# A fused attention, expert and SoLU kernel: w_gate split in six steps, weight conversion one chunk later, and other PSUM banks for the last block's first matmul

## The chip, the cores and the metric

The kernel runs on one core of a Trainium2 chip. The metric is the device time of one execution in microseconds, and runs are compared by their median. The engines are named as in the profile: PE (matmul) with PEld (its weight loads), DVE (VectorE), ACT (ScalarE), POOL (GpSimd) and SP, which here issues the DMAs. Each engine works through its own queue in order: an instruction that waits holds everything behind it on that engine.

## The reference, cut to what matters

Three layers follow each other. Attention with random features works on 4 batches, 8 heads, 576 positions and 128 features. Its output x (2304 tokens by 512) goes through a gate that picks one of 8 experts for each token. The result goes through a SoLU layer.

```python
def _attn_ref(q, k, v, omega):
    q_p, k_p = phi(q_s), phi(k_s)              # exp of a projection less its maximum
    kv = np.einsum('bhsm,bhsd->bhmd', k_p, v)
    num = np.einsum('bhsm,bhmd->bhsd', q_p, kv)
    return num / den

def _moe_ref(x, w_gate, w1, w2):
    logits = x @ w_gate
    expert_idx = np.argmax(logits, axis=1)
    for e in range(E):
        h = np.maximum(xe @ w1[e], 0.0)
        out[mask] = gate_w[mask, None] * (h @ w2[e])

def _moe2_ref(x, w_in, w_out, g_ln):
    h = x @ w_in                               # then softmax * h, layer norm
    return (ln @ w_out).astype(np.float32)
```

## The kernel before, in words

Every fp32 operand of a large matmul is split into two fp16 parts, high and low, and a product is three matmuls: high by high, high by low, low by high. ACT makes the high part, DVE or POOL the low part by a subtraction.

The work has three strands, each a Python generator whose pieces are placed by hand in the order of the program. Strand A (`stream_a`) is the attention: units of 128 positions and half of the heads, pipelined over a few units. A unit's projection `pj` goes to PSUM, DVE takes its negative maximum `nm` (L213), ACT takes the exponential `feat` (L219), and DVE and ACT split it into `fh` and `fl`. Strand B (`phase_b(b)`, b from 0 to 3) computes one batch's expert layer, under the assumption that all its tokens take the expert of its first token (a fallback repairs the tokens that do not). Its first matmul, here called g1, has 16 passes of 12 matmuls; each pass fills one PSUM bank with 128 by 288 results, which ACT writes as `hh` (L646) and DVE as the remainder `hl` (L647). Its second matmul, g2, has 8 passes of 24 matmuls, whose results ACT writes to `yT` (L652). Strand C is the SoLU layer at the end, whose first two tiles (`c_start`) start inside block 3.

Before strand B begins, strand A runs alone for some slots (a slot is one unit of strand A). A table `pre` hangs other work on single slots, among it `wg_split` on slot 9: it scales w_gate by its largest absolute value (over partitions by a matmul with a tile of ones, `wgs`) and splits it into `wg`, which the routing matmul `rt` (L337) reads in later slots.

The weights of strand C come as 64-bit words. Sixteen chunks of 128 by 512 are loaded (`craw`), repacked to 32 bits by three DVE instructions (L606, L607, L609, into `ctmp`), scaled by ACT (L625), rounded by ACT (L626, `wih` or `woh`), and the remainder is made by POOL (L62, `wil` or `wol`). `craw` and `ctmp` have two buffers each. `cw_split(k)` does this in three steps, and one step is taken after each step of strand B from the middle of block 2 on. The order within one step of strand B is: the PE pass, the evacuation of the pass before it (`flush`), the splitting of expert weights (`wh` L557, `wl` L558), then the step of `cw_split`, and in block 3 what `first_c` holds (`y_early` makes `yc` on ACT and POOL).

Banks for g1 and g2 come from `b_bank`. Once strand A has ended it alternates two pools of two banks, so a pass waits for the evacuation of the pass four before it:

```python
        if cps and count[0] % 2:
            return cps["t"].tile([128, cs.stop - cs.start], F32, name=name, tag="lt")
        return bpsum.tile([128, cs.stop - cs.start], F32, name=name, tag="b")
```

Passes of block 3's g1 are numbered 0 to 15 below, and hh(n) and hl(n) are the evacuation of pass n. They are issued after the matmuls of pass n+1.

Of the kernel before, what the change touches and what calls it, by code (L numbers as in the profile page):

```python
# [8 lines left out]
F32 = mybir.dt.float32  # L9
# [4 lines left out]
AF = mybir.ActivationFunctionType  # L14
# [6 lines left out]
B, H, S, D, M = 4, 8, 576, 64, 128  # L21
# [35 lines left out]
def f32(ap):  # L57
    return ap.bitcast(F32)


def sub(eng, out, a, b):
    eng.tensor_tensor(out=out, in0=a, in1=b, op=ALU.subtract)  # L62
# [3 lines left out]
def attn_moe_solu(ctx: ExitStack, tc, qk0, qT, kT, v, omT, w_gate, w1, w2, w_in, w_out, g_ln, out):  # L66
    nc = tc.nc
    pe, act, dve, pool, sp = nc.tensor, nc.scalar, nc.vector, nc.gpsimd, nc.sync
# [98 lines left out]
    def split_v(b, t):  # L167

        r = vparts[b, t] = vraws.pop((b, t))
        if t < 4:  # L170
            act.activation(v_h[:, t, :, 0:64], r, AF.Copy, scale=VS)
        else:
            for o in range(2):
                p, hs = slice(64 * o, 64 * o + 64), slice(4 * o, 4 * o + 4)
                act.activation(v_h[p, t, hs, 0:64], r[p, hs], AF.Copy, scale=VS)

    def split_v_lo(b, t):
        r = vparts.pop((b, t))
        if t < 4:
            dve.scalar_tensor_tensor(v_l[:, t], r, VS, v_h[:, t, :, 0:64], op0=ALU.mult, op1=ALU.subtract)  # L180
        else:
            for o in range(2):
                p, hs = slice(64 * o, 64 * o + 64), slice(4 * o, 4 * o + 4)
                dve.scalar_tensor_tensor(v_l[p, t, hs], r[p, hs], VS, v_h[p, t, hs, 0:64],
                                          op0=ALU.mult, op1=ALU.subtract)
# [374 lines left out]
    def pump(limit, due=0):  # L560

        state["calls"] += 1
        while state["split"] < min(limit, state["dma"]):
            i = state["split"]
            if i >= due and state["calls"] - sent[i] < 2:
                break
            chunk_split(i)
            state["split"] += 1
        while state["dma"] < min(max(state["split"] + NRAW, 8), len(chunks)) and chunks[state["dma"]][0] in ereg:
            chunk_dma(state["dma"])  # L570
            sent[state["dma"]] = state["calls"]
            state["dma"] += 1
# [3 lines left out]
    cs_ = {}  # L576
    rooms = {}
# [15 lines left out]
    def cw_dma(k):  # L593
        if k >= 16:
            return
        if k < 8:
            c, hf = divmod(k, 2)
            src = w_in[c * 128:c * 128 + 128, hf * 512:hf * 512 + 512]
        else:
            src = w_out[(k - 8) * 128:(k - 8) * 128 + 128, :]  # L600
        sp.dma_start(cs_["raw"][:, k % 2], src.bitcast(I32).rearrange("p (f t) -> p f t", t=2))

    def words32(w, raw):

        lo, hi = raw[:, :, 0], raw[:, :, 1]
        dve.tensor_scalar(w, hi, 3, 0x3FFFFFF8, op0=ALU.logical_shift_left, op1=ALU.bitwise_and)  # L606
        dve.scalar_tensor_tensor(w, hi, -0x40000000, w, op0=ALU.bitwise_and, op1=ALU.bitwise_or)  # L607
        yield
        dve.scalar_tensor_tensor(w, lo, 29, w, op0=ALU.logical_shift_right, op1=ALU.bitwise_or)  # L609

    def cw_split(k):

        if k < 8:
            c, hf = divmod(k, 2)
            h, l = [cw[n][:, c, hf * 512:hf * 512 + 512] for n in ("wih", "wil")]
            g = WS
        else:
            h, l = [cw[n][:, k - 8, :] for n in ("woh", "wol")]
            g = g_ws[:, k - 8:k - 7]
        w = cs_["w"][:, k % 2]  # L620
        yield from words32(w, cs_["raw"][:, k % 2])
        cw_dma(k + 2)
        yield
        w = f32(w)
        act.activation(w, w, AF.Copy, scale=g)  # L625
        act.copy(h, w)  # L626
        sub(pool, l, w, h)
        yield

    cps = {}  # L630
    count = [0]

    def b_bank(b, name, cs):
        count[0] += 1
        if cps and count[0] % 2:
            return cps["t"].tile([128, cs.stop - cs.start], F32, name=name, tag="lt")
        return bpsum.tile([128, cs.stop - cs.start], F32, name=name, tag="b")

    def phase_b(b):
        xh, xl = xTs[b]  # L640
        hh = bp.tile([128, 8, S], F16, name="hh", tag="hh")
        hl = bp.tile([128, 8, S], F16, name="hl", tag="hl")
        todo = []

        def evac_h(ps, ft, cs):
            act.activation(hh[:, ft, cs], ps, AF.Relu)  # L646
            dve.scalar_tensor_tensor(hl[:, ft, cs], ps, 0.0, hh[:, ft, cs], op0=ALU.max, op1=ALU.subtract)  # L647

        def evac_y(ps, dt, cs):
            if dt == 0 and cs.start == 0:  # L650
                yTs[b] = ypool.tile([128, 4, S], F32, name="yT", tag=f"y{b}")
            act.activation(yTs[b][:, dt, cs], ps, AF.Copy, scale=YS / (XS * BS * BS))  # L652

        def flush():
            while todo:
                todo.pop(0)()

        c0 = 16 * b
        halves = (slice(0, 256), slice(256, S)) if b == 0 else (slice(0, HS), slice(HS, S))
        if b == 0:  # L660
            passes = [(ft, cs) for cs in halves for ft in range(8)]
        else:
            passes = [(ft, cs) for ft in range(8) for cs in halves]
        for n, (ft, cs) in enumerate(passes):
            if (b, ft) not in wt:
                pump(c0 + ft + 1, c0 + ft + 1)
            wh, wl = wt[b, ft]
            ps = b_bank(b, "g1", cs)
            for c in range(4):
                pe.matmul(ps, wh[:, c, :], xh[:, c, cs], start=(c == 0), stop=False)  # L670
                pe.matmul(ps, wh[:, c, :], xl[:, c, cs], start=False, stop=False)  # L671
                pe.matmul(ps, wl[:, c, :], xh[:, c, cs], start=False, stop=(c == 3))  # L672
            flush()
            todo.append(lambda ps=ps, ft=ft, cs=cs: evac_h(ps, ft, cs))
            pump(c0 + ft + 5 if b else (n + 3 if n < 6 else 9 + max(0, n - 12)))
            yield
        for dt in range(4):
            if (b, 9 + 2 * dt) not in wt:
                pump(c0 + 10 + 2 * dt, c0 + 10 + 2 * dt)
            ww = [wt[b, 8 + 2 * dt], wt[b, 9 + 2 * dt]]  # L680
            for s, cs in enumerate(halves):
                ps = b_bank(b, "g2", cs)
                for k in range(8):
                    wh, wl = ww[k // 4]
                    if k == 7:
                        flush()
                    pe.matmul(ps, wh[:, k % 4, :], hh[:, k, cs], start=(k == 0), stop=False)  # L687
                    pe.matmul(ps, wh[:, k % 4, :], hl[:, k, cs], start=False, stop=False)  # L688
                    pe.matmul(ps, wl[:, k % 4, :], hh[:, k, cs], start=False, stop=(k == 7))  # L689
                    if k == 3:  # L690
                        flush()
                        pump(c0 + 8 + 2 * dt + 5)
                        yield
                todo.append(lambda ps=ps, dt=dt, cs=cs: evac_y(ps, dt, cs))
                pump(c0 + 8 + 2 * dt + 5 + s)
                yield
        flush()
# [342 lines left out]
    for o in range(2):  # L1040
        p, cs = slice(64 * o, 64 * o + 64), slice(128 * o, 128 * o + 128)
# [12 lines left out]
        if live[0] and next(a, a) is a:  # L1054
            live[0] = False

    def wg_split():

        dve.tensor_reduce(lgs[:, 0:1], wg_raw, axis=AX.XY, op=ALU.max, apply_absolute_value=True)
        ps = bpsum.tile([128, 512], F32, name="wgs", tag="b")  # L1060
        pe.matmul(ps[:, 0:1], ones, lgs[:, 0:1], start=True, stop=True)
        dve.tensor_scalar(lgs[:, 1:2], ps[:, 0:1], 2.0 ** -14, 1e-30, op0=ALU.mult, op1=ALU.max)
        dve.reciprocal(lgs[:, 0:1], lgs[:, 1:2])
        dve.tensor_scalar(wg_raw, wg_raw, lgs[:, 0:1], None, op0=ALU.mult)
        dve.tensor_scalar(lgs[:, 1:2], lgs[:, 1:2], 1.0 / XS, None, op0=ALU.mult)
        dve.tensor_copy(wg[:, 0], wg_raw)
        dve.tensor_tensor(wg[:, 1], wg_raw, wg[:, 0], op=ALU.subtract)

    split_v(0, 0)
    pre = {0: lambda: (split_pair(0, "k", 2), split_v_lo(0, 0), load_v(0, 3), split_v(0, 1)),  # L1070
           1: lambda: (split_pair(0, "k", 3), split_v_lo(0, 1), load_v(0, 4), split_v(0, 2)),
           2: lambda: (split_pair(0, "k", 4), split_v_lo(0, 2), split_v(0, 3)),
           3: lambda: (split_v_lo(0, 3), split_v(0, 4)),
           4: lambda: split_v_lo(0, 4),
           9: wg_split}
    slot = 0
    while x_done.get(0, -1) < 1:
        a_half()
# [15 lines left out]
    def c_start(k):  # L1094
# [4 lines left out]
    first_c = {3: lambda: y_early(0), 7: lambda: y_early(1), 11: lambda: y_early(2), 15: lambda: y_early(3),  # L1099
               23: lambda: c_start(0), 25: lambda: next(ms[0]), 26: lambda: next(ms[0]),  # L1100
               27: lambda: c_start(1), 29: lambda: next(ms[1]), 30: lambda: next(ms[1])}
    cwg = (_ for k in range(16) for _ in cw_split(k))
    for b in range(B):
        while b and x_done.get(b, -1) < 4:
            a_half()
# [88 lines left out]
```

## Time and profile before

| what | value |
|---|---|
| median of 3 runs | 562.1 us (561.03 to 564.17) |
| the profiled execution | 563.37 us, its span 561.5 us |
| busy share of the span | PE 90%, DVE 77%, ACT 60%, POOL 11% |
| chain that ended last | PE 50%, DVE 21%, ACT 11%, DMA 7% |

Sums about the change are made against the profiled execution: 561.5 us of span and 1.87 us outside it. That execution lies 1.3 us above the median. The 90% for PE is a mean over stages: in the first stage (strand A alone) PE is idle a good part of the time, in most of strand B and C it is busy throughout.

### The profile page before, as it was taken

How to read it: one execution, taken by the hardware profiler on the slowest of the kernel's cores; microseconds unless marked ns; L12 is line 12 of the kernel's file. 1: busy time of each engine (PE TensorE's matmuls, PEld its weight loads, DVE VectorE, ACT ScalarE, POOL GpSimd, SP SyncE). 2: the span in 40 equal slices, each digit the busy share in tenths (PEclk: the TensorE clock that was granted, in tenths of full speed). 3: DMA queues.
4: the chain of work that ended last, by engine and by line, in shares of the span. 5: the costliest groups of instructions: out<-in, count | busy, mean ns of one | idle time of the engine just before them, and what ended most of it. 6: DMA issues, size and time to landing. Idle time of an engine off the chain costs nothing.

```text
span 561.5 us, 11966 instructions
## 1 busy us (share of the span) xinstructions
PE 506.7 (90%) x4440; PEld 344.8 (61%) x4440; DVE 432.3 (77%) x926; ACT 339.3 (60%) x769; POOL 63.0 (11%) x86
## 2 busy tenths in 40 slices
PE   6878698797988999989989978999999999999995
PEld 2557576586867878868877756664444444444443
DVE  5978877588978988677886777767699988778670
ACT  6768468687777867666654564534474646655520
POOL 4210000000000000000012143221112121211200
PEclk8998989798999999999999999999999999999999
DMA  7405664626663455521556454505777776676741
GB/s 252 114 2 175 185 177 109 180 54 208 174 189 108 135 159 146 159 78 57 169 170 183 141 176 135 167 0 151 206 188 206 195 207 161 180 195 149 152 112 42
DMA packets 80143, 83.50 MB, mean 149 GB/s; under 512 B 43728, under 2 KB 50512, under 8 KB 80080
## 3 DMA queue, kind: packets, MB, share of 16 engines
q1 hardware_dynamic: 80080, 82.69, 51.9%
q8 instruction: 36, 0.59, 0.4%
q14 instruction: 27, 0.22, 0.1%
HBM read 56.71 MB, written 9.44 MB: 118 GB/s over the span
## 4 chain that ended last, share of the span: by engine, by line
PE 50%; DVE 21%; ACT 11%; DMA 7%; issue 6%; SPq 3%; POOL 1%; ACTq 0%; DVEq 0%; POOLq 0%
PE h L743 5%; PE o L810 5%; PE o L812 5%; PE o L811 5%; PE h L741 5%; PE h L742 5%; ACT feat L219 4%; DVE nm L213 4%; PE g L687 3%; PE g L688 3%; PE g L689 3%; PE g L670 2%; PE g L672 2%; PE g L671 2%; DMA vraw<-in_v_dram 2%
## 5 line engine op out<-in xcount | busy, mean ns | idle before, releaser
L219 ACT ACTIVATE feat<-pj,nm 128x128 f32<-128x128 f32 x288 | 82.7, 377 | 40.4 <-DVE nm L213 37.9
L670 PE MATMUL g<-xh,wh 128*128 128x288 f16 (+2 forms) x224 | 64.6, 288 | 12.3 <-DVE hl L647 11.7
L687 PE MATMUL g<-hh,wh 128*128 128x288 f16 (+2 forms) x256 | 74.3, 290 | 1.4 <-DVE hl L647 1.4
L688 PE MATMUL g<-hl,wh 128*128 128x288 f16 (+2 forms) x256 | 74.4, 290 | 0.4 <-DVE hl L647 0.4
L689 PE MATMUL g<-hh,wl 128*128 128x288 f16 (+2 forms) x256 | 74.4, 290 | 0.0
L672 PE MATMUL g<-xh,wl 128*128 128x288 f16 (+2 forms) x224 | 64.6, 288 | 0.0
L671 PE MATMUL g<-xl,wh 128*128 128x288 f16 (+2 forms) x224 | 64.6, 288 | 0.0
L810 PE MATMUL o<-woh,lh 128*128 128x512 f16 (+1 forms) x152 | 55.9, 368 | 0.3 <-ACT ob L813 0.3
L812 PE MATMUL o<-woh,ll 128*128 128x512 f16 (+1 forms) x152 | 55.9, 368 | 0.0
L811 PE MATMUL o<-wol,lh 128*128 128x512 f16 (+1 forms) x152 | 55.9, 368 | 0.0
L558 DVE SCALAR_TENSOR_TENSOR wl<-wraw,wh 128x512 f16<-128x512 f32 x56 | 42.3, 756 | 12.2 <-ACT wh L557 8.9
L213 DVE TENSOR_REDUCE nm<-pj 128x4 f32<-128x512 f32 x72 | 49.0, 681 | 1.9 <-PE pj L199 1.0
L743 PE MATMUL h<-wih,yl 128*128 128x512 f16 x112 | 42.5, 379 | 0.7 <-POOL yl L62 0.7
L647 DVE SCALAR_TENSOR_TENSOR hl<-g,hh 128x288 f16<-128x288 f32 (+2 forms) x64 | 28.8, 451 | 18.0 <-ACT hh L646 18.0
L741 PE MATMUL h<-wih,yh 128*128 128x512 f16 x112 | 42.5, 379 | 0.0
L742 PE MATMUL h<-wil,yh 128*128 128x512 f16 x112 | 42.4, 379 | 0.0
L237 DVE SCALAR_TENSOR_TENSOR fl<-feat,fh 128x512 f16<-128x512 f32 x36 | 27.3, 758 | 16.3 <-ACT fh L233 15.2
L62 POOL TENSOR_TENSOR wil<-ctmp,wih 128x512 f16<-128x512 f32 x8 | 9.3, 1158 | 272.2 <-ACT wih L626 272.2
L557 ACT ACTIVATE wh<-wraw 128x512 f16<-128x512 f32 x56 | 35.7, 638 | 3.6 <-PE g L688 3.6
L838 ACT ACTIVATE wck<-wck 128x2048 f32<-128x2048 f32 x16 | 30.5, 1904 | 12.2 <-DMA wck<-in_w_dram 12.2
L207 PE MATMUL pj<-ws,stk 128*128 128x128 f16 x216 | 31.3, 224 | 4.5 <-DMA stk<-hlp 3.4
L751 DVE TENSOR_REDUCE sc<-h 128x1 f32<-128x1024 f32 x18 | 21.9, 1218 | 16.8 <-PE h L743 16.8
(183 smaller groups left out, 1231.6 us busy)
## 6 DMA issues: line engine op xcount, KB each, us to landing
wck<-in_w_dram SPq DMA_DIRECT2D x16, 1024.0 KB, 6.0
wraw<-in_w_dram SPq DMA_DIRECT2D x56, 256.0 KB, 2.8
stk<-hlp SPq DMA_DIRECT2D x96, 72.0 KB, 2.3
out_dram<-ob SPq DMA_DIRECT2D x17, 256.0 KB, 2.2
vraw<-in_v_dram SPq DMA_DIRECT2D x16, 256.0 KB, 4.6
xd<-x SPq DMA_DIRECT2D x16, 256.0 KB, 3.5
craw<-in_w_in_dram SPq DMA_DIRECT2D x8, 512.0 KB, 4.1
craw<-in_w_out_dram SPq DMA_DIRECT2D x8, 512.0 KB, 3.3
```

The source lines that it names most:

```text
L213: dve.tensor_reduce(nm, ps, axis=AX.X, op=ALU.max, negate=True)
L219: act.activation(f[:, i, :], ps[:, i, :], AF.Exp, bias=nm[:, i:i + 1])
L670: pe.matmul(ps, wh[:, c, :], xh[:, c, cs], start=(c == 0), stop=False)
L671: pe.matmul(ps, wh[:, c, :], xl[:, c, cs], start=False, stop=False)
L672: pe.matmul(ps, wl[:, c, :], xh[:, c, cs], start=False, stop=(c == 3))
L687: pe.matmul(ps, wh[:, k % 4, :], hh[:, k, cs], start=(k == 0), stop=False)
L688: pe.matmul(ps, wh[:, k % 4, :], hl[:, k, cs], start=False, stop=False)
L689: pe.matmul(ps, wl[:, k % 4, :], hh[:, k, cs], start=False, stop=(k == 7))
L741: pe.matmul(ps[:, n, :], h[:, c, :], cw["wih"][:, c, cs], start=(c == 0), stop=False)
L810: pe.matmul(ps, h[:, k, :], cw["woh"][:, k, cs], start=(k == 0), stop=False)
L811: pe.matmul(ps, h[:, k, :], cw["wol"][:, k, cs], start=False, stop=False)
L812: pe.matmul(ps, l[:, k, :], cw["woh"][:, k, cs], start=False, stop=(k == 7))
```

## The change

The change has three parts. First, `wg_split` becomes a generator of six steps on slots 6 to 11. Second, `words32` gives up control after each of its DVE instructions, and the ACT and POOL part of a chunk's conversion is put on a list and issued in the second step of the next chunk; the load of the chunk after next moves to the third step. Third, in block 3 the passes 7, 9, 11, 13 and 15 of g1 take halves (one bank each) of two-bank tiles `h` of the pool that strand C uses for its own first matmul.

```diff
         dve.tensor_scalar(w, hi, 3, 0x3FFFFFF8, op0=ALU.logical_shift_left, op1=ALU.bitwise_and)
+        yield
         dve.scalar_tensor_tensor(w, hi, -0x40000000, w, op0=ALU.bitwise_and, op1=ALU.bitwise_or)
         yield
         dve.scalar_tensor_tensor(w, lo, 29, w, op0=ALU.logical_shift_right, op1=ALU.bitwise_or)
...
-        yield from words32(w, cs_["raw"][:, k % 2])
+        for _ in words32(w, cs_["raw"][:, k % 2]):
+            yield
+            for part in cw_parts:
+                cw_parts.pop()()
         cw_dma(k + 2)
-        yield
-        w = f32(w)
-        act.activation(w, w, AF.Copy, scale=g)
-        act.copy(h, w)
-        sub(pool, l, w, h)
-        yield
+
+        def parts():
+            wf = f32(w)
+            act.activation(wf, wf, AF.Copy, scale=g)
+            act.copy(h, wf)
+            sub(pool, l, wf, h)
+
+        cw_parts.append(parts)
+        yield
+
+    cw_parts = []
...
-    def b_bank(b, name, cs):
+    def b_bank(b, name, cs, spare=False):
         count[0] += 1
+        if cps and b == B - 1 and name == "g1" and spare:
+            if count[0] % 4 == 0:
+                rooms["g1"] = cps["h"].tile([128, 2, 512], F32, name="h")
+            if count[0] % 4 in (0, 2) and "g1" in rooms:
+                return rooms["g1"][:, count[0] % 4 // 2, 0:cs.stop - cs.start]
...
-            ps = b_bank(b, "g1", cs)
+            ps = b_bank(b, "g1", cs, n > 4)
...
-    def wg_split():
+    def wg_steps():
 
         dve.tensor_reduce(lgs[:, 0:1], wg_raw, axis=AX.XY, op=ALU.max, apply_absolute_value=True)
+        yield
         ps = bpsum.tile([128, 512], F32, name="wgs", tag="b")
         pe.matmul(ps[:, 0:1], ones, lgs[:, 0:1], start=True, stop=True)
+        yield
         dve.tensor_scalar(lgs[:, 1:2], ps[:, 0:1], 2.0 ** -14, 1e-30, op0=ALU.mult, op1=ALU.max)
         dve.reciprocal(lgs[:, 0:1], lgs[:, 1:2])
+        yield
         dve.tensor_scalar(wg_raw, wg_raw, lgs[:, 0:1], None, op0=ALU.mult)
+        yield
         dve.tensor_scalar(lgs[:, 1:2], lgs[:, 1:2], 1.0 / XS, None, op0=ALU.mult)
         dve.tensor_copy(wg[:, 0], wg_raw)
+        yield
         dve.tensor_tensor(wg[:, 1], wg_raw, wg[:, 0], op=ALU.subtract)
-
+        yield
+
+    wgs = wg_steps()
...
-           9: wg_split}
+           **{6 + k: lambda: next(wgs) for k in range(6)}}
...
-    cwg = (_ for k in range(16) for _ in cw_split(k))
+    def cw_all():
+        for k in range(16):
+            yield from cw_split(k)
+        yield
+        cw_parts.pop()()
+
+    cwg = cw_all()
```

On DVE, around slot 9 of the start, the order moves like this (`lgs` holds the maximum and its reciprocal, `wg_raw` is w_gate, `kvl` and `nm` belong to strand A):

```order
-L1059 TENSOR_REDUCE lgs<-wg_raw 128x1
-L1062 TENSOR_SCALAR lgs<-wgs 128x1
-L1063 RECIPROCAL lgs<-lgs 128x1
-L1064 TENSOR_SCALAR wg_raw<-wg_raw,lgs 128x32
-L1065 TENSOR_SCALAR lgs<-lgs 128x1
-L1066 CAST wg<-wg_raw 128x32
-L1067 TENSOR_TENSOR wg<-wg_raw,wg 128x32
-L213 TENSOR_REDUCE nm<-pj 128x4
+L1081 TENSOR_SCALAR wg_raw<-wg_raw,lgs 128x32
+L213 TENSOR_REDUCE nm<-pj 128x4
+L1083 TENSOR_SCALAR lgs<-lgs 128x1
+L1084 CAST wg<-wg_raw 128x32
```

Seven instructions stood in front of this `nm`, and one is left there. The reduction has gone to slot 6, the next two to slot 8, two stand behind the `nm`, and the last has gone to slot 11.

On ACT, at the start of block 3, the instructions up to hh(0) and hh(1) before (`g1_5715` and `g1_5738` are the banks of passes 0 and 1, `ex` belongs to the gates):

```order
L652 ACTIVATE yT_5280<-g2_5664 128x288 [waits PE_49]
L557 ACTIVATE wh_5728<-wraw_5594 128x512 [waits DMAHW5_49]
L358 ACTIVATE ex_5707<-ex_5707,lgs_86 64x8 [waits DVE_49]
L625 ACTIVATE ctmp_115<-ctmp_115 128x512 [waits DVE_49]
L626 CAST wih_110<-ctmp_115 128x512 [waits Activation_49]
L646 ACTIVATE hh_5713<-g1_5715 128x288 [waits PE_49]
L646 ACTIVATE hh_5713<-g1_5738 128x288 [waits PE_49]
```

The same stretch in the changed kernel (banks `g1_5713` and `g1_5735`):

```order
L666 ACTIVATE yT_5280<-g2_5662 128x288 [waits PE_49]
L630 ACTIVATE ctmp_115<-ctmp_115 128x512 [waits DVE_49]
L631 CAST wih_110<-ctmp_115 128x512 [waits Activation_49]
L557 ACTIVATE wh_5726<-wraw_5592 128x512 [waits DMAHW4_49]
L358 ACTIVATE ex_5703<-ex_5703,lgs_86 64x8 [waits DVE_49]
L660 ACTIVATE hh_5711<-g1_5713 128x288 [waits PE_49]
L660 ACTIVATE hh_5711<-g1_5735 128x288 [waits PE_49]
```

The two conversion instructions now stand ahead of `wh` and `ex`, and they belong to the chunk before: nothing of the conversion stands directly in front of hh(0).

On PE, the first matmul of passes 7 to 13 of block 3's g1 before:

```order
L670 MATMUL g1_5865<-xh_5050,wh_5696 128x288 [waits DVE_49]
...
L670 MATMUL g1_5884<-xh_5050,wh_5728 128x288 [waits DVE_49]
...
L670 MATMUL g1_5907<-xh_5050,wh_5728 128x288 [waits DVE_49]
...
L670 MATMUL g1_5925<-xh_5050,wh_5773 128x288 [waits DVE_49]
...
L670 MATMUL g1_5948<-xh_5050,wh_5773 128x288 [waits DVE_49]
...
L670 MATMUL g1_5967<-xh_5050,wh_5816 128x288 [waits DVE_49]
...
L670 MATMUL g1_5991<-xh_5050,wh_5816 128x288 [waits DVE_49]
```

And in the changed kernel:

```order
L684 MATMUL h_5862<-xh_5050,wh_5693 128x288
...
L684 MATMUL g1_5880<-xh_5050,wh_5726 128x288 [waits DVE_49]
...
L684 MATMUL h_5862<-xh_5050,wh_5726 128x288 [waits DVE_49]
...
L684 MATMUL g1_5921<-xh_5050,wh_5769 128x288
...
L684 MATMUL h_5943<-xh_5050,wh_5769 128x288 [waits PE_49]
...
L684 MATMUL g1_5964<-xh_5050,wh_5813 128x288 [waits DVE_49]
...
L684 MATMUL h_5943<-xh_5050,wh_5813 128x288 [waits DVE_49]
```

Passes 7 and 11 open a tile `h` and wait for no evacuation. Passes 9 and 13 fill the second half of that tile and do wait for DVE.

## Rows read from the trace of the kernel before

**Rows 1.** The start: us; busy PE, PEld, DVE, ACT, POOL; clock, DMA share, GB/s

```profile
22.00:28.00 6.00, 5.09 (x72) 3.63 (x70) 5.69 (x10) 4.29 (x15) 2.38 (x2) 1.00 0.00 0
```

**Rows 2.** Timeline of DVE at slots 9 and 10: start, duration (us), instruction, [idle before, releaser]

```profile
29.86 0.69 DVE L237 SCALAR_TENSOR_TENSOR fl<-feat,fh 128x512 f16<-128x512 f32 x1
30.47 0.18 DVE L1059 TENSOR_REDUCE lgs<-wg_raw 128x1 f32<-128x32 f32 x1
31.12 0.16 DVE L1062 TENSOR_SCALAR lgs<-wgs 128x1 f32<-128x1 f32 x1 [0.47 <-PE wgs L1061]
...
31.51 0.92 DVE L1064 TENSOR_SCALAR wg_raw<-wg_raw,lgs 128x32 f32<-128x32 f32 x1
...
32.47 0.18 DVE L1066 CAST wg<-wg_raw 128x32 f16<-128x32 f32 x1
32.68 0.19 DVE L1067 TENSOR_TENSOR wg<-wg_raw,wg 128x32 f16<-128x32 f32 x1
32.79 0.68 DVE L213 TENSOR_REDUCE nm<-pj 128x4 f32<-128x512 f32 x1
35.04 0.43 DVE L261 SCALAR_TENSOR_TENSOR kvl<-kv,kvh 128x260 f16<-128x260 f32 x1 [1.57 <-ACT kvh L260]
```

**Rows 3.** Timeline of ACT behind that `nm`

```profile
33.59 1.14 ACT L219 ACTIVATE feat<-pj,nm 128x128 f32<-128x128 f32 x4 [2.43 <-DVE nm L213]
```

**Rows 4.** Timeline of POOL at slot 9

```profile
31.24 1.16 POOL L62 TENSOR_TENSOR stk<-raw,stk 128x512 f16<-128x512 f32 x1 [2.97 <-ACT stk L135]
```

**Rows 5.** Block 3's g1, the same columns

```profile
311.50:342.30 30.80, 24.85 (x194) 18.72 (x193) 23.36 (x44) 17.99 (x39) 10.51 (x9) 1.00 0.48 161
```

**Rows 6.** Waits from 312 to 350 us: total, times, longest

```profile
ACT ctmp L625 <- DVE ctmp L609: 13.0, 6, 2.7
DVE hl L647 <- ACT hh L646: 7.7, 6, 1.9
...
PE g L670 <- DVE hl L647: 6.0, 7, 1.6
```

**Rows 7.** Timeline of ACT in block 3's g1

```profile
316.18 0.63 ACT L625 ACTIVATE ctmp<-ctmp 128x512 f32<-128x512 f32 x1 [0.43 <-DVE ctmp L609]
...
317.37 0.70 ACT L646 ACTIVATE hh<-g 128x288 f16<-128x288 f32 x2
...
327.86 0.72 ACT L625 ACTIVATE ctmp<-ctmp,g_ws 128x512 f32<-128x512 f32 x1 [2.49 <-DVE ctmp L609]
```

**Rows 8.** Timeline of DVE: hl(0), hl(3), hl(6), hl(9), hl(11)

```profile
317.81 0.46 DVE L647 SCALAR_TENSOR_TENSOR hl<-g,hh 128x288 f16<-128x288 f32 x1 [1.05 <-ACT hh L646]
...
323.76 0.46 DVE L647 SCALAR_TENSOR_TENSOR hl<-g,hh 128x288 f16<-128x288 f32 x1 [1.81 <-ACT hh L646]
...
329.57 0.46 DVE L647 SCALAR_TENSOR_TENSOR hl<-g,hh 128x288 f16<-128x288 f32 x1 [0.78 <-ACT hh L646]
...
335.63 0.46 DVE L647 SCALAR_TENSOR_TENSOR hl<-g,hh 128x288 f16<-128x288 f32 x1 [1.38 <-ACT hh L646]
...
339.85 0.44 DVE L647 SCALAR_TENSOR_TENSOR hl<-g,hh 128x288 f16<-128x288 f32 x1
```

**Rows 9.** Instructions of line L607: ns least/median/most, first and last start

```profile
L607 DVE SCALAR_TENSOR_TENSOR ctmp<-craw,ctmp x16: 692/693/1534, 274.0 to 362.2; 128x512 int32<-128x512 int32 x16
```

**Rows 10.** Timeline of PE: first matmul of block 3's g1, and two of g2

```profile
311.52 0.29 PE L670 MATMUL g<-xh,wh 128*128 128x288 f16 x1
...
345.57 0.28 PE L688 MATMUL g<-hl,wh 128*128 128x288 f16 x1 [0.39 <-DVE hl L647]
...
354.51 0.29 PE L689 MATMUL g<-hh,wl 128*128 128x288 f16 x1
```

**Rows 11.** Timeline of PE in the last third of block 2

```profile
279.14 0.28 PE L687 MATMUL g<-hh,wh 128*128 128x288 f16 x1 [0.93 <-DVE hl L647]
...
291.64 0.19 PE L337 MATMUL rt<-wg,xh 128*128 128x8 f16 x2 [1.95 <-DVE rd L294]
```

**Rows 12.** The loads of `craw`, from issue to landing

```profile
DMA to landing us min/median/max: 3.1/3.7/5.7
```

## The prediction

> **What bounds the kernel now.** The page comes first: PE is busy 90% of the span, so a gain has to come from stretches in which PE waits. The chain that ended last gives DVE 21% and ACT 11%, and its pieces in order of time lie in two places that the change touches: the start, where it runs through the seven w_gate instructions, and block 3's g1, where it alternates between the repacking on DVE and the scaling on ACT. So I read the timelines there.
>
> At the start, DVE is the engine without gaps: from 22 to 28 us, slots 6 to 8, it is busy 5.69 of 6 us [rows 1]. Its `fl` ends at 30.55; then come the reduction, a wait of 0.47 for the small matmul, two short instructions, `wg_raw` with 0.92, and three short ones; `nm` is entered once the last of them has ended, at 32.87 [rows 2]. ACT sits idle 2.43 us until that `nm` is there [rows 3], and what follows is a chain of `feat`, `kvl` and the next `nm`. So 32.87 - 30.55 = 2.3 us lie on the chain.
>
> In block 3's g1 the view of waits shows a circle. ACT waits 13.0 us for the last repacking instruction, DVE waits 7.7 us for hh, PE waits 6.0 us for hl [rows 6]. ACT's queue explains it: it reaches the scaling of a chunk before DVE has finished repacking that chunk, stands there (2.49 us in one place), and the next hh stands behind it [rows 7]. What PE loses is clearer from its starts. From 345.57 to 354.51 it starts 73 matmuls after the first without a wait, 0.1225 us each, so a g1 pass takes 1.47 us [rows 10]. From the start of g1 at 311.52 to the matmul at 345.57 (the 23rd of g2's first pass, the one that reads hl(14)) there are 192 + 22 steps, 26.2 us of work in 34.05 us: PE loses 7.8 us [rows 10]. The granted clock is 1.00 there [rows 5], so none of this is the clock.
>
> **The change part by part.**
>
> *w_gate in six steps.* On slot 6 the reduction costs 0.18 on DVE; the small matmul on slot 7 finds its operand long ready, so the 0.47 goes away; on slot 8 the two short instructions cost 0.39 (31.12 to 31.51) [rows 2]. These three still lie on the chain, since DVE has no gaps there. On slot 10 two instructions (0.25, from the end of `wg_raw` at 32.43 to 32.68) come right behind `nm`, where DVE idles 1.57 us before `kvl` [rows 2]: free, and 0.25 if that gap were gone. The last one (0.19) goes to slot 11, where I give it the same nothing, at worst 0.19. What remains is `wg_raw` on slot 9. It has 128 by 32 elements like the cast (0.18), yet took 0.92 [rows 2], and POOL ran its subtraction from 31.24 to 32.40 over it [rows 4]. In the new order it starts at once after `fl`, which with 0.57 of earlier steps ends at 31.1, and POOL's subtraction, pushed by the same 0.57, starts near 31.8. I take 0.18. Sum on the chain: 0.18 + 0.39 + 0.18 = 0.75 instead of 2.3, a gain of 1.6 us. With POOL over it, 0.92, the gain is 0.8.
>
> The Trainium skill, page "GPSIMD Engine Reference", section 1 (Specifications), says that GpSimd shares its SBUF interfaces with VectorE, and that a VectorE instruction with two SBUF inputs or in a two-port mode contends with it. The rows agree: 0.92 beside POOL against 0.18. By the rule a subtraction on POOL at that moment costs the 0.74 again, by the row's timing it comes too late for that.
>
> *Conversion one chunk later, end of block 2.* Nothing is added or removed: 16 chunks with the same six instructions and one load. In DVE's new order, one repacking instruction of 0.69 [rows 9] moves from in front of an hl to behind it, and another from in front of the remainder of x that the routing waits for. PE waits at these two places 0.93 and 1.95 us [rows 11]. Bounds: nothing, if the wait is really for ACT, and 2.9 if both waits vanish. I take 0.69 less some overlap twice, 1.3 us.
>
> *Conversion one chunk later, block 3.* Before hh(0) stood 0.43 of waiting and 1.19 us of scaling and rounding (316.18 to 317.37) [rows 7]; in the new order neither does, so hl(0) starts 1.6 earlier, at 316.2 instead of 317.81 [rows 8]. After that ACT meets a scaling whose repacking DVE issued two steps earlier. DVE then becomes the bound: from hl(0) to the end of hl(11) at 340.29 it took 22.5 us, 1.81 + 0.78 + 1.38 = 4.0 of them idle waiting for hh [rows 8], so 18.5 us of work, while PE's passes up to 13 need 13 x 1.47 = 19.1 from 311.52 [rows 10].
>
> *The banks.* Pass 9 and pass 13 write the second bank of a tile whose first bank was filled two passes before, and the order shows both waiting for DVE, while passes 10, 14 and 15 show no wait at all although they take over banks from passes 6, 10 and 9. A wait on hl(7) and hl(11) covers all of these, so I read it as a wait for the whole tile. It replaces one for hl(5) and hl(9): two passes of room where four were. So pass 13 cannot start before hl(11) is done, at 316.2 + 18.5 = 334.7, or by PE's own count at 330.6. From there 58 steps (36 + 22) of 0.1225, 7.1 us, lead to the matmul at 345.57 [rows 10]: 341.8 or 337.7, a gain of 3.8 or 7.8. Which it is depends on DVE's 18.5. They hold stretching beside POOL, which runs nine instructions in the stage [rows 5]: L607 takes 0.69 alone and up to 1.53 [rows 9]. All nine remain, so I stay near the lower end and take 5.0.
>
> The Trainium skill, page "PSUM — Partial Sum Buffer", Summary: rules for kernel authors, says to let a matmul write another bank than the one that is read, with semaphores guarded by bank. By bank, pass 13 would wait for nothing, and only pass 15 would wait, for hl(11): 34 steps or 4.2 us before the matmul in question, 338.9, a gain of 6.7. The order shows a wait by tile, so I do not use it.
>
> *What else moves.* The load of a chunk is issued in the third step, so it has four steps, 4 x 1.47 = 5.9 us, instead of five until it is read; it takes 3.7 us, at most 5.7 [rows 12]: free, barely. The last chunk ends two steps later, beside g2, where PE runs without a wait [rows 10]: free, and its 1.2 us of ACT if that cover were gone. PE has two more banks and two fewer waits in passes 7 and 11, which is inside the sum above. Behind block 3 everything follows in order, so I carry the gain to the end.
>
> Sum: 1.6 + 1.3 + 5.0 = 7.9 us. Against the profiled execution that is a span of 553.6 and a time of 555.5; against the median of 562.1 it is 554.2. I say 555.0 us, between them.
>
> **The rivals.**
>
> *The banks and DVE take most of it back.* If ACT still starves DVE around passes 9 and 13, where PE now stands until the evacuation of two passes ago is through, each of these two waits can cost 2 us of the 5.0. For it: the wait is in the order, and DVE is busy 23.4 of 30.8 us already [rows 5]. Against it: at pass 9 DVE still has hl(8) and two repacking instructions to do. Time: 562.1 - 1.6 - 1.3 - 1.0 = 558.2.
>
> *PE runs through.* If POOL's stretching falls elsewhere, block 3 gives 7.8 and the end of block 2 gives 2.5: 562.1 - 1.6 - 2.5 - 7.8 = 550.2 at the extreme, 552 if one of the two holds. For it: DVE's 18.5 us are just below PE's 19.1.
>
> *No change.* The steps could fall on a chain that is as tight in other slots, and the phase behind block 3 could be bound by loads. Then 561 to 562. Against it: ACT's wait of 2.43 [rows 3] has no other cause in the rows.
>
> *Slower.* The load of a chunk comes too late, DVE stands at the first repacking instruction, and every hl behind it stands too. The cover is 5.9 us against 3.7 at the median [rows 12]; it decides once a landing takes 5.9 + 7.9/16 = 6.4 us on average, above the longest seen. At 6.9, 16 chunks x 1.0 = 16 us are lost: 562.1 - 7.9 + 16 = 570.2.
>
> **How the numbers follow.** Forecast 0.55 (552.5 to 557.5), banks and DVE 0.17 (557.5 to 559.3), PE runs through 0.08 (550 to 552.5), no change 0.14 (559.3 to 564.9), slower 0.06. A change under 0.5%, 2.8 us, can't be told from none here. So faster 0.80, same 0.14, slower 0.06. The range of 552.0 to 560.4 leaves out the slower case, the extreme of the good one and most of no change, about 0.19 together.
>
> **What would show it.** Right: at the start one w_gate instruction of 0.2 us in front of that `nm`, and ACT's 2.43 shorter by 1.6; in block 3's g1 ACT's wait for L609's successor near 2 us instead of 13.0, hl(0) 1.6 us closer to the start of g1, PE losing about 3 us instead of 7.8, most of it in front of passes 9 and 13. Wrong: `wg_raw` again at 0.9; waits at the first repacking instruction for a load or for POOL; PE losing 6 us or more in g1; or a gain at the end of block 3 that is smaller at the end of the span.

## The result, and the profile after

| what | before | after |
|---|---|---|
| median, runs side by side | 562.25 us (561.03 to 566.21, 5 runs) | 556.96 us (555.48 to 557.88, 5 runs) |
| profiled execution, time and span | 563.37, 561.5 us | 556.96, 555.2 us |
| rt, first routing matmul, starts at | 45.75 us | 43.92 us |
| block 1's g1 | 39.12 us | 41.49 us |
| block 2, from its g1 to block 3's g1 | 70.48 us | 68.77 us |
| block 3's g1 | 30.80 us | 27.46 us |
| block 3's g2, up to its last matmul with hh | 34.31 us | 33.75 us |

The ratio is 0.9891, with a 95% interval of 0.986 to 0.9921: faster, by 1.1%, less than the 1.3% forecast. The stage times are differences of the first matmul's start of each stage on PE. Two of the twelve executions of e3 below, its profiled one among them, ran at a lower granted clock and over 1.5% longer than its fastest; its ratio leaves them out, and of that profile only waits and DMA issues are read.

The start, timeline of DVE in the changed kernel:

```profile
30.23 0.69 DVE L237 SCALAR_TENSOR_TENSOR fl<-feat,fh 128x512 f16<-128x512 f32 x1
30.84 0.23 DVE L1081 TENSOR_SCALAR wg_raw<-wg_raw,lgs 128x32 f32<-128x32 f32 x1
30.98 0.68 DVE L213 TENSOR_REDUCE nm<-pj 128x4 f32<-128x512 f32 x1
...
33.22 0.43 DVE L261 SCALAR_TENSOR_TENSOR kvl<-kv,kvh 128x260 f16<-128x260 f32 x1 [1.40 <-ACT kvh L260]
```

ACT behind that `nm`, the same kernel:

```profile
31.76 1.14 ACT L219 ACTIVATE feat<-pj,nm 128x128 f32<-128x128 f32 x4 [0.22 <-DVE lgs L1083]
```

And POOL:

```profile
31.62 1.22 POOL L62 TENSOR_TENSOR stk<-raw,stk 128x512 f16<-128x512 f32 x1 [3.23 <-ACT stk L135]
```

One w_gate instruction of 0.23 us is left in front of the `nm`; it took 0.92 in [rows 2]. POOL's subtraction starts 0.55 us after it has ended; in [rows 4] it ran over it. ACT's 2.43 us of [rows 3] are 0.22.

The end of block 2, timeline of PE, the two places of [rows 11]:

```profile
278.21 0.28 PE L701 MATMUL g<-hh,wh 128*128 128x288 f16 x1 [0.20 <-DVE hl L661]
...
289.72 0.19 PE L337 MATMUL rt<-wg,xh 128*128 128x8 f16 x2 [1.18 <-DVE rd L294]
```

0.93 has become 0.20 and 1.95 has become 1.18: 1.5 us of waiting less, and 1.7 us less for block 2.

Block 3's g1 and the first pass of g2, PE of the changed kernel (start of g1, passes 6, 9 and 13, start of g2, the matmul that reads hl(14)):

```profile
309.60 0.29 PE L684 MATMUL g<-xh,wh 128*128 128x288 f16 x1
...
319.48 0.28 PE L684 MATMUL g<-xh,wh 128*128 128x288 f16 x1 [0.89 <-DVE hl L661]
...
326.47 0.28 PE L684 MATMUL h<-xh,wh 128*128 128x288 f16 x1 [2.42 <-DVE hl L661]
...
332.65 0.28 PE L684 MATMUL h<-xh,wh 128*128 128x288 f16 x1
...
337.06 0.29 PE L701 MATMUL g<-hh,wh 128*128 128x288 f16 x1
...
339.75 0.29 PE L702 MATMUL g<-hl,wh 128*128 128x288 f16 x1
```

DVE in the same stretch, hl(0), hl(7), hl(11) and hl(14):

```profile
314.43 0.46 DVE L661 SCALAR_TENSOR_TENSOR hl<-g,hh 128x288 f16<-128x288 f32 x1
...
325.98 0.44 DVE L661 SCALAR_TENSOR_TENSOR hl<-h,hh 128x288 f16<-128x288 f32 x1
...
332.14 0.46 DVE L661 SCALAR_TENSOR_TENSOR hl<-h,hh 128x288 f16<-128x288 f32 x1 [0.32 <-ACT hh L660]
...
337.15 0.45 DVE L661 SCALAR_TENSOR_TENSOR hl<-g,hh 128x288 f16<-128x288 f32 x1
```

Pass 9 starts 0.05 us after hl(7) has ended at 326.42, and pass 13 starts 0.05 after hl(11) at 332.60. So the second bank of a tile does wait for the evacuation of the first one. From g1's start to the matmul with hl(14) it is 339.75 - 309.60 = 30.15 us instead of 34.05: 3.9 us won. That matmul does not wait for its operand: hl(14) had ended at 337.60, 2.15 us earlier.

The waits from 310 to 348 us (total, times, longest):

```profile
ACT ctmp L630 <- DVE ctmp L610: 5.2, 4, 2.4
...
PE h L684 <- DVE hl L661: 2.4, 1, 2.4
...
PE g L684 <- DVE hl L661: 0.9, 1, 0.9
...
DVE hl L661 <- ACT hh L660: 0.3, 1, 0.3
DVE ctmp L606 <- DMA craw<-in_w_out_dram: 0.2, 1, 0.2
```

The circle of [rows 6] is gone: DVE waits 0.3 us for hh instead of 7.7. Busy times of g1, columns as in [rows 5]:

```profile
309.60:337.06 27.46, 24.01 (x195) 18.77 (x193) 26.84 (x47) 19.35 (x41) 11.56 (x10) 1.00 0.59 185
```

DVE is busy 26.84 of 27.46 us: up to hl(11) it is the bound of this stage now. Behind hl(11) PE runs its remaining steps without a wait.

One loss that the prediction does not speak of lies elsewhere, in block 1's g1, which took 2.4 us more than before. Its windows (columns as in [rows 5]):

```profile
195.00:198.00 3.00, 1.29 (x21) 1.04 (x19) 1.13 (x3) 1.28 (x3) 0.00 (x0) 1.00 0.71 211
198.00:201.00 3.00, 2.81 (x22) 2.29 (x22) 2.84 (x9) 1.85 (x7) 0.00 (x0) 0.71 0.44 117
201.00:204.00 3.00, 3.00 (x30) 2.79 (x29) 2.07 (x6) 2.93 (x7) 0.00 (x0) 0.72 0.38 105
```

Then what ACT and PE waited for there:

```profile
196.72 0.63 ACT L171 ACTIVATE v_h<-vraw 128x512 f16<-128x512 f32 x1 [2.64 <-DMA vraw<-in_v_dram]
```

```profile
198.19 0.28 PE L684 MATMUL g<-xh,wh 128*128 128x288 f16 x1 [1.90 <-DVE hl L661]
```

ACT waits 2.64 us for a load of strand A (1.88 before), an hh stands behind it, then an hl, and PE idles 1.90 us (1.15 before). After that the granted clock is 0.71 and 0.72 in the two windows of three microseconds; in before it was 1.00 behind the shorter wait. So part of these six microseconds ran at 1.2 GHz instead of 2.4. Nothing in this stage was edited.

### The profile page after: what moved, and what is told of

It is laid out like the page before. It is cut to its first block, busy times and chain, and to the rows that moved or that the text cites. A ratio compares the mean times of both kernels' runs of the same rounds, so it can differ in the third digit from the quotient of the medians.

```text
span 555.2 us, 11967 instructions
## 1 busy us (share of the span) xinstructions
PE 505.2 (91%) x4440; PEld 344.9 (62%) x4440; DVE 434.5 (78%) x926; ACT 339.8 (61%) x769; POOL 66.2 (12%) x86
## 4 chain that ended last, share of the span: by engine, by line
PE 53%; DVE 20%; ACT 9%; DMA 8%; issue 5%; SPq 3%; POOL 1%; DVEq 0%; ACTq 0%; POOLq 0%
PE h L757 5%; PE o L824 5%; PE o L826 5%; PE o L825 5%; PE h L755 5%; PE h L756 5%; PE g L701 4%; DVE nm L213 4%; PE g L703 4%; PE g L702 4%; ACT feat L219 3%; PE g L684 2%; PE g L686 2%; PE g L685 2%; DMA vraw<-in_v_dram 2%
## 5 line engine op out<-in xcount | busy, mean ns | idle before, releaser
L684 PE MATMUL g<-xh,wh 128*128 128x288 f16 (+2 forms) x204 | 59.5, 292 | 6.5 <-DVE hl L661 5.9
L686 PE MATMUL g<-xh,wl 128*128 128x288 f16 (+2 forms) x204 | 59.8, 293 | 0.0
L685 PE MATMUL g<-xl,wh 128*128 128x288 f16 (+2 forms) x204 | 59.6, 292 | 0.0
L660 ACT ACTIVATE hh<-g 128x288 f16<-128x288 f32 (+2 forms) x59 | 24.9, 422 | 16.8 <-PE g L686 16.6
```

## The experiments

Each of the three parts alone, the first two together, and then two questions on what bounds block 3 and two on what the banks cost.

**e1_wg: the w_gate steps alone**, the first part of the change, made to the kernel before.

> Only the w_gate steps; conversion and banks as before. Theory: the start gains what it gained in the changed kernel (routing's first matmul at 43.9 instead of 45.8 us, 1.9 us earlier) and the rest follows, so about 560.4 against 562.3. Rival: what the start gains is taken back between 160 and 205 us, where the changed kernel waits longer for a load of v and the clock falls; then block 2's g1 starts at 241 us as before and the time is 562.

Measured: 560.23 us (12 runs, 557.92 to 565.24) against 562.93, ratio 0.9955 (0.9923 to 0.9988). ACT behind that `nm`:

```profile
31.26 1.14 ACT L219 ACTIVATE feat<-pj,nm 128x128 f32<-128x128 f32 x4 [0.22 <-DVE lgs L1069]
```

The matmul with hl(14) starts at 343.81 instead of 345.57, so 1.76 us of the start's gain still stand after 340 us. The median is 2.7 us below before's: the gain is carried to the end. Over all profiles rt starts at 43.42 to 44.35 us in the nine kernels with the steps and at 45.52 to 45.85 in the three without them.

**e2_lag: the later conversion alone**, the second part, made to the kernel before.

> Only the conversion one chunk later; w_gate and banks as before. Theory: ACT's wait for the last repacking instruction is what held block 3, so g1 of block 3 falls from 30.8 to about 26 us (DVE, always busy, ends hl(14) 22.5 to 23.5 us after hl(0)), and the end of block 2 gains 1 to 1.7: 555.5 to 557. Rival: the banks bring the gain of block 3, and then g1 stays near 30 and the time near 560.5.

Measured: 555.26 us (6 runs, 554.56 to 558.25), ratio 0.9859 (0.981 to 0.9907); block 3's g1 25.74 us, block 2 37.36 + 31.40 = 68.76. The gain in block 3 is the conversion's, and the old banks get more of it than the new ones (27.46).

**e3_banks: the banks alone**, the third part, made to the kernel before.

> Only the other banks; w_gate and conversion as before. Theory: no gain, g1 of block 3 stays at 30.8 or takes up to 2 us more, because passes 9 and 13 wait for the evacuation of two passes before: 562 to 564. Rival (the banks bring the gain): g1 27.5, time 559.

Measured: 564.5 us (12 runs, 560.38 to 569.93), ratio 1.0004 (0.9969 to 1.0039): nothing gained. Timeline of PE, passes 8 and 9:

```profile
331.25 0.28 PE L675 MATMUL g<-xh,wh 128*128 128x288 f16 x1 [2.18 <-DVE hl L652]
...
336.69 0.40 PE L675 MATMUL h<-xh,wh 128*128 128x288 f16 x1 [2.87 <-DVE hl L652]
```

With the old circle between ACT and DVE still there, pass 9 waits for the tile as it does in the changed kernel: hl(7) had ended at 336.65. Pass 7, which opens a tile, no longer waits (0.63 us before), but pass 8 waits longer for it (2.18 instead of 1.38).

**e4_wg_lag: w_gate steps and later conversion, old banks.** The changed kernel with this undone:

```diff
-            ps = b_bank(b, "g1", cs, n > 4)
+            ps = b_bank(b, "g1", cs)
```

> The changed kernel with the old banks. Theory: the wait on the whole tile goes, pass 15 waits for hl(11) instead of pass 13, and the matmul that reads hl(14) comes when DVE has it, 2 us earlier than in the changed kernel: g1 of block 3 at 25.5 to 26 instead of 27.5, time 555. Rival: the banks are worth something, g1 28.5 or more, time 558 or more.

Measured: 552.44 us (6 runs, 551.83 to 553.39), ratio 0.9803 (0.9758 to 0.9848); block 3's g1 25.73 us. Its waits of PE there, passes 6 and 10 and the matmul with hl(14):

```profile
316.21 0.28 PE L679 MATMUL g<-xh,wh 128*128 128x288 f16 x1 [0.89 <-DVE hl L656]
...
322.51 0.28 PE L679 MATMUL g<-xh,wh 128*128 128x288 f16 x1 [0.26 <-DVE hl L656]
...
335.31 0.28 PE L697 MATMUL g<-hl,wh 128*128 128x288 f16 x1 [0.39 <-DVE hl L656]
```

No 2.42 us anywhere, and the matmul with hl(14), the last line, waits for hl(14) itself. The time is 2.6 us below the 555 expected; in e10 below the same kernel took 554.36. The windows of g1, and the costliest groups of DVE in it (count, busy us and mean ns):

```profile
306.34:332.07 25.73, 24.16 (x194) 18.75 (x192) 25.49 (x44) 17.69 (x38) 10.76 (x9) 1.00 0.53 174
```

```profile
L558 DVE SCALAR_TENSOR_TENSOR wl<-wraw,wh 128x512 f16<-128x512 f32 x8 | 8.0, 995 | 0.2 <-ACT wh L557 0.2
L608 DVE SCALAR_TENSOR_TENSOR ctmp<-craw,ctmp 128x512 int32<-128x512 int32 x5 | 7.9, 1587 | 0.0
```

DVE has 0.24 us to spare, and one repacking instruction takes 1587 ns in the mean, where it took 1026 before and 693 at the median in [rows 9].

**e5_six: e4_wg_lag with six single banks in rotation**, so that no wait is for half a tile.

```diff
+        if cps and b == B - 1 and name == "g1" and count[0] % 3 == 0:
+            return cps["h"].tile([128, 2, 512], F32, name="h")[:, 0, 0:cs.stop - cs.start]
+        if cps and b == B - 1 and name == "g1":
+            n = count[0] % 3 == 1
...
```

> w_gate steps and later conversion as in the changed kernel, but block 3's g1 rotates over three pools with one bank a tile, so that a pass waits for the pass six before and no wait on a two-bank tile is left. Theory: DVE, which has no gaps from hl(0) to hl(14), is the bound, so two more banks are worth nothing against the old four: g1 plus the lead-in to the matmul that reads hl(14) ends as in the run with the old banks (hl(14) 22.5 to 23 us after hl(0)), time 552 to 553. Rival: room in PSUM is what counts, and six banks bring 1.5 us or more beyond the old four, 551 or less.

Measured: 553.71 us (6 runs, 550.75 to 556.94), ratio 0.9873 (0.9828 to 0.9919). Block 3's g1 takes 25.75 us, as with four banks. PE does not wait once inside g1, but in front of g2:

```profile
332.40 0.28 PE L702 MATMUL g<-hh,wh 128*128 128x288 f16 x1 [2.07 <-DVE hl L662]
332.53 0.28 PE L703 MATMUL g<-hl,wh 128*128 128x288 f16 x1
...
333.05 0.45 PE L703 MATMUL g<-hl,wh 128*128 128x288 f16 x1
333.29 0.45 PE L704 MATMUL g<-hh,wl 128*128 128x288 f16 x1
```

More room only moves the wait to where the room ends, since DVE delivers at its own pace. The steps behind the wait are 0.24 us instead of 0.1225, and g2 up to its last matmul with hh takes 35.43 us, where e4 needs 34.30. This profile also has the longer g1 of block 1 (41.52 us), so its time says nothing against the four banks; the stage times do not show any gain from six.

**e6_nopool: e4_wg_lag without POOL's remainders.** It leaves out the low parts `wil` and `wol` of strand C's weights, which are set to zero once at the start of the conversion.

```diff
-            sub(pool, l, wf, h)
+            pass
...
```

> w_gate steps, later conversion, old banks; the remainders wil and wol of strand C's weights are left out (set to zero once), so 16 POOL subtractions of 1.2 us are missing and the output lacks the low part of the weights. Theory: DVE's instructions with two SBUF inputs are stretched (0.69 to 1.6 us) when POOL runs over them, and DVE is the bound, so without five of nine POOL instructions in the stage DVE gets about 3 us shorter and g1 of block 3 falls from 25.7 to 24 us or less, time 550.5. Rival: the stretching falls where DVE has time, g1 stays at 25.5 or more.

Measured: 550.75 us (6 runs, 550.17 to 552.75), ratio 0.9822 (0.9787 to 0.9857). Block 3's g1 takes 23.52 us, which is 16 passes of 1.47: PE never waits. The windows of g1 and two groups of DVE:

```profile
307.20:330.73 23.53, 23.53 (x194) 18.79 (x192) 22.22 (x48) 19.43 (x41) 4.23 (x3) 1.00 0.67 218
```

```profile
L558 DVE SCALAR_TENSOR_TENSOR wl<-wraw,wh 128x512 f16<-128x512 f32 x9 | 6.4, 708 | 0.5 <-ACT wh L557 0.5
L612 DVE SCALAR_TENSOR_TENSOR ctmp<-craw,ctmp 128x512 int32<-128x512 int32 x6 | 4.1, 681 | 0.0
```

The same repacking instruction (here L612) takes 681 ns instead of 1587. The share of DMA is higher here (0.67 against 0.53), so the loads are not what stretches it. POOL's work is not on the path by itself; what it does to DVE is. The ratio is no better than e4's, though: the 2.2 us of this stage are less than what separates runs on different chips (e4's kernel has 0.9876 as e10 below).

**e7_dvesub: e4_wg_lag with these remainders on DVE.**

```diff
-            sub(pool, l, wf, h)
+            sub(dve, l, wf, h)
```

> w_gate steps, later conversion, old banks; the remainders wil and wol are made on DVE instead of POOL. Theory: DVE gains the stretching of about 0.8 us per POOL instruction and pays 0.65 us for each, so it is about the same or a little better in block 3's g1 (25 to 26 us), time 552 to 553. Rival: DVE is so full that the added 16 x 0.65 us show, g1 27 us or more and 555 or more.

Measured: 553.11 us (6 runs, 551.99 to 553.64), ratio 0.9851 (0.9817 to 0.9885); block 3's g1 25.62 us. The two groups of DVE there:

```profile
L608 DVE SCALAR_TENSOR_TENSOR ctmp<-craw,ctmp 128x512 int32<-128x512 int32 x6 | 4.1, 682 | 0.0
...
L62 DVE TENSOR_TENSOR wil<-ctmp,wih 128x512 f16<-128x512 f32 x3 | 3.0, 1006 | 0.0
...
L62 DVE TENSOR_TENSOR wol<-ctmp,woh 128x512 f16<-128x512 f32 x2 | 1.4, 680 | 0.0
```

Five subtractions come on top, 4.4 us, and the repacking gets back 3.8 (7.9 to 4.1) and `wl` 1.1 (8.0 to 6.9). On POOL the work costs DVE about as much as if DVE did it, and the stage is as long (25.62 against 25.73 us).

**e8_one, e9_changed, e10_wg_lag: where block 1's 2.4 us belong, and the price of the banks side by side.** e9 is the changed kernel and e10 is e4_wg_lag, on one chip. e8 is e4_wg_lag with this:

```diff
+        if cps and b == B - 1 and name == "g1" and n == 15:
+            return cps["h"].tile([128, 2, 512], F32, name="h")[:, 0, 0:cs.stop - cs.start]
```

> w_gate steps and later conversion as in e4_wg_lag, and one bank of a tile h for the last pass of block 3's g1 alone. Pass 15 then waits for no evacuation; passes 0 to 14 are as in e4_wg_lag. What is asked is block 1's g1, far ahead of the edit: 41.3 to 41.5 us in the three kernels so far whose last g1 uses tiles h, 38.9 to 39.2 in the six that do not. If the 2.4 us come with any use of these tiles, block 1's g1 is 41.4 here and the time 555; if they come with executions, or with more of the edit than this, it is 39.0 and the time 552.5. Block 3's g1 25.5 to 26 in both.

> The changed kernel again, beside e10_wg_lag on one chip, so that the price of the banks is measured directly. If the 2.4 us of block 1 belong to the program, block 1's g1 is 41.5 us again and the time is 557, 4.5 above e10_wg_lag; if they belonged to one profiled execution, it is 39.0 and the time is 1.7 to 2 above e10_wg_lag, which is what block 3's g1 (27.46 against 25.73) accounts for.

> w_gate steps and later conversion with the old banks again, the same kernel as e4_wg_lag, as the other half of that comparison. Block 1's g1 39.0 us and block 3's g1 25.7 by either theory; 552.4 us.

Measured against 559.79 us of before: e8 552.75 us (549.2 to 553.15, 4 runs), ratio 0.9828 (0.9749 to 0.9906); e9 555.08 us (554.02 to 556.41, 4 runs), 0.9883 (0.981 to 0.9956); e10 554.36 us (553.47 to 555.12, 4 runs), 0.9876 (0.9804 to 0.9948). Block 1's g1 took 39.31, 38.86 and 39.14 us. In e9 ACT waited for that load so:

```profile
197.06 0.63 ACT L171 ACTIVATE v_h<-vraw 128x512 f16<-128x512 f32 x1 [1.62 <-DMA vraw<-in_v_dram]
```

```profile
198.53 0.28 PE L684 MATMUL g<-xh,wh 128*128 128x288 f16 x1 [0.89 <-DVE hl L661]
```

The same program has 1.62 and 0.89 us here, 2.64 and 1.90 in the first profile. So the program does not bring the 2.4 us along each time. Whether the bank edit makes them likelier is open: three of the four profiles in which several passes use tiles `h` have the long wait for that load (2.64 us in the first of the changed kernel, 2.48 in e3, 2.67 in e5, but not e9), and none of the eight others (2.09 at most). In block 3 nothing differs between the two profiles of the changed kernel: g1 takes 27.45 us, pass 9 waits 2.43. From g1's start to g2's last matmul with hh e9 needs 27.45 + 33.76 = 61.21 us and e10 25.74 + 34.29 = 60.03. In block 3 the banks cost 1.2 us, 0.2%. The two medians are 0.7 us apart with overlapping runs, so by time alone this price can't be resolved.

## Why the prediction was right, and by how much not

The direction and the cause were right, the measured median lies 2.0 us above the forecast and inside its range. Term by term, in e9's profile, which the wait in block 1 doesn't disturb: span 554.0 us, 7.5 less than before, where the sum said 7.9. These are single executions: by medians the gain is 5.3 us in the first comparison and 4.7 in e9's. The profiled execution of before (563.37 us) lies above both medians of before (562.25 and 559.79), which makes the difference of the spans look larger. That the sum came so near is in part luck: the first two terms were about half a microsecond too small together, and the third was 1.1 too large.

- *w_gate, 1.6 us.* It measured 1.83 in the first profile (rt at 43.92 instead of 45.75) and 1.75 in e9. The choice of 0.18 for `wg_raw` rested on POOL's subtraction coming too late; it came 0.55 us too late. e1 shows that the gain is carried to the end. The rival of no change, that the chain is as tight in other slots, does not hold.
- *End of block 2, 1.3 us.* It measured 1.7. Both waits shrank by about one repacking instruction, 0.73 and 0.77, as the two places of 0.69 said; no overlap had to be taken off.
- *Block 3, 5.0 us: this term was mis-sized; it measured 3.9.* Its working held step by step. hl(0) came 4.83 us after g1's start (4.7 forecast), from hl(0) to the end of hl(11) it took 332.60 - 314.43 = 18.17 us (18.5), so pass 13 started 23.05 us after g1's start, where "by DVE's 18.5" the text had 334.7 - 311.52 = 23.2. That way gave 3.8, the lower bound. That the 18.5 held is itself in part luck: between these two hl the stretching of DVE's instructions grew by 1.2 us, while one repacking instruction less lay there. What failed is the choice above the bound, "I stay near the lower end and take 5.0": nothing of DVE's stretching fell away. In this stage L608 took 1281 ns in the mean, more than the 1026 of before. That POOL is what stretches it, e6 and e7 show. DVE also met POOL more often: of its 128x512 instructions with two SBUF inputs 5 of 18 ran beside one of POOL's in this stage before, and 11 of 19 in the changed kernel; what they took above 0.69 us each rose from 3.3 to 5.8 us in sum. Why they meet more often was not tested.
- *The banks.* The text priced them only inside that term and not by themselves. e4_wg_lag shows what the same conversion gives with four old banks: its matmul with hl(14) comes at 335.31 - 306.34 = 28.97 us, a gain of 5.1. The new banks take 1.2 of it. In the changed kernel pass 13 waits for hl(11) with 58 steps still to go, and the matmul comes 2.15 us after its hl(14). In the old order the pass that needs hl(11) is pass 15, with 34 steps to go; it starts at 330.16, 0.3 us after hl(11) has ended, and so only hl(14) itself holds the matmul.
- *By bank or by tile.* The Trainium skill, page "PSUM — Partial Sum Buffer", Summary: rules for kernel authors, wants semaphores guarded by bank; by that rule the text worked out 6.7 us. The rows show the wait by tile, 2.42 us in front of pass 9, and 3.9. This wait stands in the program; no run guards the two halves apart, so what that would give is not shown. The working by bank also named the wrong pass: by the prediction's own list pass 15 takes over the tile of passes 7 and 9, so by bank the last wait would have been pass 14's, for hl(10).
- *What would show it.* PE lost 3.9 us in g1 (27.46 - 23.52) instead of the 3 named, 2.9 of it in front of passes 9 and 13 and 1.1 in front of pass 6. ACT's wait for L609's successor is 5.2 us, not 2: it still reaches some scalings early, but DVE no longer waits behind it (0.3).
- *The rivals.* "Slower" needed loads of 6.4 us; DVE waited for one 0.2 us once. "The banks and DVE take most of it back" had its mechanism right, and its price at pass 9 (2 us, measured 2.42), but by pass 13 PE had only 0.3 more to wait. "PE runs through" needed DVE below PE's 19.1 without stretching: in e6 it is so, with 7.28 us of g1 given back (30.80 - 23.52).

In the first profile of the changed kernel the span is 6.3 us shorter. The three terms give 7.4 there, block 1's g1 takes 2.4 back, and 1.2 come from small differences ahead of block 1 and behind block 3. No step of the prediction speaks of block 1, and e9 shows that the program doesn't always make it so: the load landed 5.3 us after its issue, in e9 4.3. What delays it stays open. In the three profiles that have the long wait SP issued the two loads behind it without a stop (0.47 and 0.59 us); in the nine one of these two issues took 1.3 to 2.0 us, so that less came beside the load. That is an observation, not a tested cause.

Of the versions with all of the reference's work e4_wg_lag, the change without the banks, has the lowest ratio (0.9803). Its times do not rank it safely: the same kernel has 0.9876 as e10, and e8 beside it 0.9828. What speaks for leaving the banks out is the 1.2 us in block 3.

## What to carry to other kernels

Price each part of a change by itself, also the part that looks like pure room: here six banks instead of four cost 1.2 us, because the wait on half of a two-bank tile covered both halves and left two passes of room where the old order left four. Where an engine has become the bound, more buffers ahead of it only move the wait (e5: out of g1, 2.07 us in front of g2); look for what stretches that engine. And where an estimate has a worked lower bound and only a hope above it, take the bound.

## What the runs showed of the hardware

- A VectorE instruction of 128 by 512 with two SBUF inputs took 681 ns with little on POOL beside it (e6) and 1587 in the mean with POOL's subtractions beside it (e4). hl, which reads PSUM, took 446 to 448 in e4, e6 and the changed kernel alike. The prediction counted on the stretching, but not on more of it than before.
- Which of the two is stretched went by the start. From the changed kernel's g1, DVE and POOL, first with POOL ahead by 0.11 us, then with DVE ahead by 0.22:

```profile
326.94 1.64 DVE L608 SCALAR_TENSOR_TENSOR ctmp<-craw,ctmp 128x512 int32<-128x512 int32 x1
326.83 1.20 POOL L62 TENSOR_TENSOR wol<-ctmp,woh 128x512 f16<-128x512 f32 x1 [2.63 <-ACT woh L631]
...
331.14 0.68 DVE L608 SCALAR_TENSOR_TENSOR ctmp<-craw,ctmp 128x512 int32<-128x512 int32 x1
331.36 1.48 POOL L62 TENSOR_TENSOR wol<-ctmp,woh 128x512 f16<-128x512 f32 x1 [3.32 <-ACT woh L631]
```

  Between 250 and 380 us of the twelve profiles, 56 of DVE's 128x512 instructions with two SBUF inputs began ahead of the one POOL instruction that they met: all took 0.66 to 0.69 us. 126 began behind it, and 124 of these took 0.92 to 1.68. So in these runs the order of the starts went with which of the two paid.
- The granted clock fell to about 0.7 after PE had idled 1.90 us (after) and 1.94 (e5) in block 1's g1; behind 2.07 us in front of g2 (e5) steps went from 0.1225 to 0.24 us, 1.2 GHz instead of 2.4. It did not fall behind the 2.42 and 2.43 us at pass 9 (1.00 from 309.60 to 337.06), nor behind the 1.95 us at the end of block 2 in [rows 11] (1.00 from 292 to 298). So the length of one idle does not tell whether it falls. What else decides it was not tried.
